# Row tiles of 128, column tiles, whole query loads, merged stores and a new tail in a cosformer and Hyena kernel

## The chip, the cores and the metric

The kernel runs on one core of a Trainium2 chip. The metric is the device time of one execution in microseconds. Runs that differ by over 1.5% from the fastest of the same kernel are called slow.

## The reference

Linear attention with a cosine weight, for 8 batches of 8 heads, 576 rows and 64 columns, and then a gate whose middle factor is a circular convolution along the rows:

```python
q_p, k_p = phi(q, cos_w, sin_w), phi(k, cos_w, sin_w)   # relu(x)*cos, relu(x)*sin side by side
kv  = einsum('bhsf,bhsd->bhfd', k_p, v);  z = k_p.sum(axis=2)
num = einsum('bhsf,bhfd->bhsd', q_p, kv)
den = einsum('bhsf,bhf->bhs', q_p, z)[..., None] + 1e-06
x   = (num / den) as (8, 576, 512)
x1, x2, x3 = split(x @ w_proj, 3)
x2_conv = irfft(rfft(x2, axis=1) * rfft(filter_fft, axis=0), axis=1)
out = (x1 * x2_conv * x3) @ w_out
```

## The kernel before

The batches are pipelined: while batch b goes through the gate, batch b + 1 gets its `num`, and batch b + 2 is loaded and prepared. Four rotating buffers serve the loads of q, k and v. From batch 2 on the prepared queries are transposed by DMA in four pieces, one for each pair of heads, so the `num` of a pair needs its own piece only. The x1/x3 input `xt` is a fifth transposing DMA. These and the stores of the output are issued from one engine, SyncE. (Cuts are marked with `# ...`.)

```python
def load_qk(b, nm, hs=slice(0, NH)):
    rw = work.tile([NP, NH, NJ * D], FP16, tag="raw", bufs=4, name=f"{nm}raw{b}")   # q, k and v
    # ... q from batch 2 on: three loads, the second half of each row with even and odd rows swapped

def emit_qt(b, hp):
    qp, qpt = qp_t[b], qpt_buf[0].rearrange("p (h n) -> p h n", h=NH)   # one qpt buffer
    hsl = slice(2 * hp, 2 * hp + 2)
    if b >= DMA_QT:
        nc.sync.dma_start_transpose(
            out=qpt[:, hsl].rearrange("p h (j n) -> p (h j) n", j=NJ),
            in_=qp[:, hsl].rearrange("p h j a b -> p (h j a b)"),
        )
        return
    # ... batches 0 and 1 on TensorE

def emit_x2(b, bls=range(3)):            # three blocks of 2 x 96 rows
    for bl in bls:
        u = unit(f"x2_{b}_{bl}")
        for comp in range(2):
            for c in range(NC):          # 8 matmuls of 96 rows x 512 columns
                nc.tensor.matmul(u[0:NP, comp], fx[:, c, ...], wp16[:, c, ds(DM, DM)], ...)
        # ... eviction on ScalarE

def emit_out(b, grps=OG):                # OT = [0, 128, 256, 384, 448]
    ov = out[b].rearrange("(k r) n -> r k n", r=12)
    # ... four matmuls for each 128 rows, eviction to os
            while pos < hi_:
                m = pos // 48
                e = min(hi_, (m + 1) * 48)       # a store has at most 48 rows of 2048 bytes
                k0, r = pos - m * 48, 6 * (m % 2) + m // 2
                q_ = nc.sync                     # ... some on other queues near the end
                q_.dma_start(out=ov[r, k0 : k0 + e - pos], in_=sv[pos - OT[t] : e - OT[t]])
                pos = e

for b in range(1, B + 1):                # n = b + 1
    # emit_x2(b, 0); num(n, 0), num(n, 1); emit_x2(b, 1); num(n, 2); dft; num(n, 3); emit_xt(n)
    # emit_x2(b, 2); dft; gates with folds of n; inverse transforms
    # loads of n + 1; phi of q (n + 1); the four emit_qt(n + 1); phi of k; copies of v
    # emit_out(b - 1); emit_kv(n + 1); emit_y(b)
```

## Time and profile before

| quantity | before |
|---|---|
| time, median of 3 runs | 254.21 us (251.4 to 259.21) |
| span of the profiled run, mean granted clock | 252.0 us, 0.970 |
| start (to the `kv` matmuls of batch 2) | 71.0 us |
| five batches, from one `kv` group to the next | 23.7, 25.0, 25.0, 25.0, 25.0 us |
| rest | 57.2 us |

The split into start, batches and rest is read from the timeline of TensorE: each batch begins its `kv` group once, and the distance of two groups (here called the pitch) is what a batch costs. The page's lines that show TensorE as the bound stand in the prediction.

First the DMA queue's own timeline for SyncE: start, time that the issue took, place, kind, transfer, count.

```profile
101.99 9.39 SPq L539 DMA_TRANSPOSE qpt<-qp  x3
111.47 4.82 SPq L617 DMA_TRANSPOSE xt<-att  x1
116.38 1.42 SPq L539 DMA_TRANSPOSE qpt<-qp  x1
```

Three of the four query pieces go ahead of `xt`, the last pair of heads behind it. The next batch's `num` begins at 122.98, and the `num` of that last pair only at 126.36, so the fourth piece has 10 us.

Second the transfers from 100 to 126 us, in 40 slices of 0.65 us: busy share of the 16 DMA engines in tenths, and GB/s.

```profile
DMA  7699999999669999999999199999999999999799
GB/s 145 39 153 221 185 143 135 235 315 214 52 133 285 238 167 89 92 187 200 236 133 68 13 215 285 291 290 224 194 189 186 184 247 32 335 413 271 44 120 162
```

Most slices are at 9: the engines are busy nearly all the time.

### The profile page before, as it was taken

Reading aid. Unit: us, or ns where it says so; the run is one execution under the profiler, and the core shown is the slowest. Engines: PE = TensorE matmul, PEld = TensorE weight load, DVE = VectorE, ACT = ScalarE, POOL = GpSimd, SP = SyncE. Lnnn points to the kernel's source line nnn. Section 1 sums busy time; section 2 is a strip of 40 time slices with the busy share of each in tenths; the row PEclk is TensorE's granted clock in tenths of the full one; section 3 lists DMA queues with packets and bytes.
Section 4 is the critical chain, followed back from the end, with each engine's and each line's share of the span. In section 5 each row is a group of like instructions: output and inputs, shape, how many; then the busy total and the mean of one; then the engine's idle time right before and its main releaser. Section 6 shows DMA issues by size and latency. Waiting matters only on the chain.

```text
span 252.0 us, 6140 instructions
## 1 busy us (share of the span) xinstructions
PE 226.1 (90%) x2313; PEld 159.9 (63%) x2313; DVE 210.4 (83%) x732; ACT 186.2 (74%) x281; POOL 38.1 (15%) x65
## 2 busy tenths in 40 slices
PE   0197897998988999999999999999999999999980
PEld 0067575655676867686768676867686778557730
DVE  7689899699779999999799979997998595828880
ACT  2244789799797876987698769876987488767720
POOL 8714211501501031103110311000000000000030
PEclk9997998899799999999999999999999999999996
DMA  5999999799999969999999999999982512153054
GB/s 68 167 205 205 207 200 153 101 166 196 173 121 157 169 56 202 174 176 194 200 225 143 141 217 199 137 183 156 161 197 53 153 41 58 44 146 83 3 153 140
DMA packets 74926, 37.30 MB, mean 148 GB/s; under 512 B 54288, under 2 KB 70160, under 8 KB 74896
## 3 DMA queue, kind: packets, MB, share of 16 engines
q0 software_dynamic: 26176, 17.21, 51.3%
q1 hardware_dynamic: 48320, 19.11, 40.6%
q10 hardware_dynamic: 400, 0.59, 0.7%
q8 instruction: 18, 0.29, 0.5%
q14 instruction: 12, 0.10, 0.2%
HBM read 33.69 MB, written 9.44 MB: 171 GB/s over the span
## 4 chain that ended last, share of the span: by engine, by line
PE 73%; DVE 13%; ACT 7%; DMA 3%; issue 1%; POOL 1%; POOLq 0%; DVEq 0%; ACTq 0%
PE x L674 21%; PE x L634 17%; PE out L752 12%; PE kv L527 5%; PE num L568 4%; PE fx L595 4%; PE dft L649 3%; DMA vraw<-in_v_dram 3%; PE inv L711 2%; PE inv L710 2%; DVE kp L104 2%; ACT va L142 1%; DVE eo L725 1%; DVE att L578 1%; PE qt L547 1%
## 5 line engine op out<-in xcount | busy, mean ns | idle before, releaser
L674 PE MATMUL x<-xt,wp 128*128 128x288 f16 x512 | 68.1, 286 | 0.0
L674 PEld LDWEIGHTS <-wp 128*128 128x128 f16 x512 | 48.9, 98 | 13.9 <-issue 0.9
L634 PE MATMUL x<-wp,fx 128*96 128x512 f16 x192 | 48.1, 395 | 1.6 <-DVE qpt L553 1.6
L752 PE MATMUL out<-wo,y 128*128 128x512 f16 x160 | 36.0, 379 | 0.1
L639 ACT ACTIVATE x2f<-x 96x1024 f16<-96x1024 f32 x24 | 24.5, 1020 | 14.2 <-PE x L634 13.9
L634 PEld LDWEIGHTS <-fx 128*96 128x96 f16 x192 | 23.0, 127 | 16.7 <-issue 3.7
L142 ACT COPY va<-vraw 96x768 f16<-96x768 f16 x32 | 25.2, 831 | 9.2 <-DMA vraw<-in_v_dram 9.2
L578 DVE TENSOR_TENSOR att<-num,rcp 96x768 f16<-96x768 f32 x32 | 30.3, 948 | 0.2
L752 PEld LDWEIGHTS <-y 128*128 128x128 f16 x160 | 15.3, 97 | 17.7 <-DVE y L730 0.6
L527 PE MATMUL kv<-va,kp 96*128 96x65 f16 x384 | 16.6, 199 | 10.2 <-ACT va L142 8.4
L684 ACT CAST x3s<-x 128x576 f16<-128x576 f32 x32 | 20.5, 641 | 5.9 <-PE x L674 5.9
L759 ACT ACTIVATE os<-out 128x1024 f32<-128x1024 f32 (+1 forms) x21 | 17.7, 880 | 9.0 <-PE out L752 8.7
L610 ACT CAST fx<-fx 128x576 f16<-128x576 f32 x32 | 20.6, 645 | 4.9 <-PE fx L595 4.9
L651 ACT CAST xf<-dft 96x1024 f16<-96x1024 f32 x24 | 24.2, 1008 | 0.0
L527 PEld LDWEIGHTS <-kp 96*128 96x128 f16 x384 | 15.1, 101 | 13.6 <-DVE kp L104 11.3
L699 DVE TENSOR_TENSOR g<-x3s,x1s 128x288 f16<-128x288 f16 x64 | 17.2, 299 | 6.8 <-ACT x3s L684 6.8
L681 ACT CAST x1s<-x 128x576 f16<-128x576 f32 x32 | 20.6, 645 | 1.8 <-PE x L674 0.8
L654 DVE TENSOR_TENSOR m<-xf,h 96x1024 f16<-96x1024 f16 x24 | 16.3, 681 | 6.1 <-ACT xf L651 5.1
L568 PEld LDWEIGHTS <-qpt 128*128 128x128 f16 (+1 forms) x384 | 16.2, 103 | 7.7 <-issue 3.9
L725 DVE TENSOR_TENSOR eo<-eq 128x288 f16<-128x288 f16 x64 | 17.5, 297 | 4.4 <-ACT eq L714 4.4
L595 PE MATMUL fx<-fm,att 96*128 96x96 f16 x240 | 17.0, 214 | 3.4 <-DVE att L578 1.7
L595 PEld LDWEIGHTS <-att 96*128 96x128 f16 x240 | 14.3, 101 | 7.6 <-DVE att L578 3.4
(192 smaller groups left out, 409.1 us busy)
## 6 DMA issues: line engine op xcount, KB each, us to landing
out_dram<-os SPq DMA_DIRECT2D x64, 96.0 KB, 2.2
kraw<-in_k_dram POOLq DMA_DIRECT2D x7, 576.0 KB, 8.6
vraw<-in_v_dram POOLq DMA_DIRECT2D x7, 576.0 KB, 8.9
qraw<-in_q_dram POOLq DMA_DIRECT2D x8, 288.0 KB, 6.0
qraw<-in_q_dram POOLq DMA_DIRECT2D x12, 144.0 KB, 5.9
wp<-in_moe_w_proj_dram POOLq DMA_DIRECT2D x3, 512.0 KB, 11.9
out_dram<-os SPq DMA_DIRECT2D x22, 64.0 KB, 2.2
out_dram<-os SPq DMA_DIRECT2D x23, 32.0 KB, 2.1
```

The lines of the kernel that those rows point to most:

```text
L142: nc.scalar.copy(out=va_buf[b % 2][:, hs, :, 0:D], in_=raw_t[(b, "v")][:, hs].rearrange("p h (j d) -> p h j d", j=NJ),)
L527: nc.tensor.matmul(u[:, h // 4, ds((h % 4) * 65, 65)], kp[:, j, h].rearrange("p a b -> p (a b)"), va[:, h, j, 0:65], start=(j == 0), stop= ...
L568: nc.tensor.matmul(u[0:m, hh, ds(t * 65, 65)], qpt[:, c0 : c0 + 2 * m - 1 : 2], kvs[:, h // 4, ds((h % 4) * 65, 65)], start=True, stop=True,)
L578: mark["att", b, hp] = nc.vector.tensor_tensor(out=att[:, :, ds(hp * 128, 128)].rearrange("p t (h d) -> p h t d", h=2), in0=nv[:, :, :, 0: ...
L595: nc.tensor.matmul(dst.rearrange("p (g e o) -> p g e o", e=2, o=8)[:, :, e], att[:, 2 * j + e, ds(c * 128, 128)], fm[0:NP, gs], start=True ...
L610: mark["fx", b] = nc.scalar.copy(out=dst[:, c].rearrange("p g (j o) -> p j g o", j=3), in_=uf[:, 0:768].rearrange("p (j g o) -> p j g o", ...
L634: nc.tensor.matmul(u[0:NP, comp], fx[:, c, ds(comp * 6 + 2 * bl, 2)].rearrange("p a b -> p (a b)"), wp16[:, c, ds(DM, DM)], start=(c == 0) ...
L639: mark["x2f", b, bl] = nc.scalar.mul(out=x2f[:, bl], in_=u[0:NP], mul=X2SC)
L651: mark["xf", b, bl] = nc.scalar.copy(out=xf, in_=u[0:NP])
L674: nc.tensor.matmul(u[:, hf, 0:HS], wp16[:, i, ds(w * DM + c * 128, 128)], xt[:, i, ds(6 * hf, 6)].rearrange("p a b -> p (a b)") if b < DMA ...
L681: mark["x1s", b, c] = nc.scalar.copy(out=x1s, in_=us[0][:, :, 0:HS])
L752: nc.tensor.matmul(u[:, x], y[:, c, ds(OT[t], 128)], wo16[:, c], start=(c == 0), stop=(c == NC - 1),)
```

## The change

The intent is to save TensorE time and to shorten the tail. x2 is computed in tiles of 128 rows, with the last 64 rows on two column halves of the array at once, and the DFT tables are padded to fit. The last 64 rows of the output are done on two column halves too. q is loaded whole into its own buffer with even and odd rows apart, and transposed in four 48-row pieces, each of which holds a part of every head. Half of the copies of v move to VectorE, and all of them later. The output's stores are merged to 96 rows where they can be, and the end of the last two batches is reordered.

```diff
+    q_buf = consts.tile([112, NH, NJ * D], FP16, tag="qraw", name="qraw")
-            rw = work.tile([NP, NH, NJ * D], FP16, tag="raw", bufs=4, name=f"{nm}raw{b}")
+            raw_t[(b, nm)] = q_buf if nm == "q" else work.tile(
+                [NP, NH, NJ * D], FP16, tag="raw", bufs=3, name=f"{nm}raw{b}"
+            )
... three loads of q become two, for even and odd rows
     def emit_qt(b, hp):
-        hsl = slice(2 * hp, 2 * hp + 2)
         if b >= DMA_QT:
+            e, half = hp % 2, hp // 2
             nc.sync.dma_start_transpose(
-                out=qpt[:, hsl].rearrange("p h (j n) -> p (h j) n", j=NJ),
-                in_=qp[:, hsl].rearrange("p h j a b -> p (h j a b)"),
+                out=qpt.rearrange("p h (j e m n) -> p (h j) e m n", j=3, e=2, m=2)[:, :, e, half],
+                in_=qp[ds(64 * ((e + half) % 2), 48), half].rearrange("p h j a b -> p (h j a b)"),
             )
... x2: two blocks of 8 matmuls with 128 rows, then
+                for c in range(2):
+                    for x in range(2):
+                        mm(u[ds(64 * x, 64), 0], 4, 64, c + 2 * x, range(2 * x, 2 * x + 2))
... DFT: nine matmuls on padded tables, not six; out: two column halves for the last 64 rows
-        ov = out[b].rearrange("(k r) n -> r k n", r=12)
+        ov = out[b].rearrange("(k x y) n -> x y k n", x=2, y=6)
-                    e = min(hi_, (m + 1) * 48)
+                    e = pos + 96 if pos % 96 == 0 and pos + 96 <= hi_ else min(hi_, (m + 1) * 48)
+                    if e - pos == 96:
+                        q_.dma_start(out=ov[:, m // 2], in_=sv[pos - OT[t] : e - OT[t]])
... order of the last batches
-            with behind("att", n, 1):
+            with behind(*("att", n, 3)):
                 emit_phi(n + 1, "k")
-                with behind(*(("x2f", b, x) if b > 1 else ("kvs", 2))):
-                    emit_va(n + 1, (2 * x, 2 * x + 1))
+                with behind("eo", b, 3):
+                    emit_va(n + 1, (0, 1))
+                with behind("g", b, 0):
+                    emit_va(n + 1, (2, 3), nc.vector.tensor_copy)
```

## The prediction

> **What bounds the kernel now.** I read the page's busy line and the chain that ended last, then the chain in order of time, which splits the run in three, then busy time by stage. Page first:
>
> ```profile
> PE 226.1 (90%) x2313; PEld 159.9 (63%) x2313; DVE 210.4 (83%) x732; ACT 186.2 (74%) x281; POOL 38.1 (15%) x65
> ...
> PE 73%; DVE 13%; ACT 7%; DMA 3%; issue 1%; POOL 1%; POOLq 0%; DVEq 0%; ACTq 0%
> ```
>
> TensorE holds 73% of the chain; the other engines' share lies at the two ends. The chain in order of time, one batch from the middle:
>
> ```profile
> 121.40 1.74 PE x L634 x8
> 123.14 0.79 PE num L568 x24
> 123.94 1.74 PE x L634 x8
> ...
> 126.92 1.75 PE x L634 x8
> ...
> 140.58 4.32 PE out L752 x20
> 144.90 1.53 PE kv L527 x48
> 146.42 1.74 PE x L634 x8
> ```
>
> A batch takes 146.42 - 121.40 = 25.02 us, every piece TensorE. A matmul of 512 columns costs 1.74/8 = 0.217 us. The work adds up: x2 24 x 0.217 = 5.2, DFT 6 x 0.216 = 1.3, gates 64 x 0.123 = 7.85 (16 in 1.96 in the chain), out 4.32, inverse 2.0, kv 1.53, num 1.58, folds 4 x 0.26 = 1.0, together 24.8. So TensorE has practically no bubble, and only fewer or shorter matmuls can help between 77 and 234 us. Busy time by stage, for two such batches, shows who is next:
>
> ```profile
> 121.40:146.42 25.02, 25.02 (x268) 18.00 (x266) 22.86 (x73) 20.84 (x30) 3.66 (x5) 1.00 1.24 178
> 146.42:171.44 25.02, 25.02 (x268) 17.99 (x266) 22.82 (x73) 20.79 (x30) 1.54 (x2) 1.00 1.21 176
> ```
>
> After the length come PE, weight loads, VectorE, ScalarE and GpSimd; then clock, DMA share, GB/s. VectorE is busy 22.8 of 25.0 us: a change can win about 2 us a batch before VectorE takes over. ScalarE has 4 us to spare. Before 77 us the chain mixes VectorE (30 to 42 us) and ScalarE (48 to 63 us); no PE saving counts there.
>
> At the end the timeline shows
>
> ```profile
> 240.67 0.46 DVE L730 TENSOR_TENSOR y<-y,g 128x576 f16<-128x576 f16 x1
> 241.18 3.35 PEld L752 LDWEIGHTS <-y 128*128 128x128 f16 x17 [0.59 <-DVE y L730]
> ...
> 245.06 0.69 DVE L102 TENSOR_SCALAR os<-out 128x512 f32<-128x512 f32 x1 [0.17 <-PE out L752]
> ```
>
> The last eviction ends at 245.75, yet the span is 252.0: 6.25 us of stores and ending. The stage table for 241 to 250 shows 111 to 271 GB/s, zero from 250 on. The transfers from 239 on are 1.84 MB, of which the last batch is 1.18: the rest are stores of the batch before, evicted as late as 239.6 to 241.1. The tail is limited by the stores' bytes, and about 2 us of ending follow.
>
> **What the Trainium skill says.** (1) "TensorE: Matmul & The Clock Gate", Back-to-back issue gap: N/2.4 + 2.5 ns when warm, 216 for 512 columns; the 0.217 agrees, and a matmul of 96 or 64 output rows costs as much as one of 128. That is what the 128-row tiles and column tiles use. (2) "TensorEngine Tiling (Array Packing)", Tiling Modes, Key Properties: tiles operate independently, but changing the tiling mode drains the engine. Before has a likely example of the drain, a weight of one column, here the weight-load timeline:
>
> ```profile
> 54.37 0.56 PEld L465 LDWEIGHTS <-hb 96*96 96x96 f16 x3
> 55.32 0.30 PEld L478 LDWEIGHTS <-alt 96*1 96x1 f16 x3 [0.40 <-issue]
> 56.06 0.12 PEld L649 LDWEIGHTS <-tre 96*96 96x96 f16 x1 [0.44 <-issue]
> ```
>
> Its load and the next one are not pulled ahead. Three matmuls from 54.58 should end issue at 55.23, h_nyq starts at 55.32; three more end at 55.97, DFT starts at 56.06. So I estimate 0.1 us a switch. That two 64-column tiles really overlap no record of before shows. (3) The clock-gate page, Part 3, "Measured speedup", gives 2.38x for three column tiles; I take nearly 2x for two. (4) "VectorE: DVE Perf Modes", perf-mode tier table: a 16-bit SBUF copy can run at 4x. The trace's like operation, the 96x768 maximum on q, takes 0.35 us.
>
> **The change part by part, per middle batch.**
>
> x2: three blocks of 8 matmuls become two of 8 and a 64-row rest in four matmuls, two on each half of the columns. The third block falls from 1.73 to 2 x 0.216 + 2 switches = 0.65, a gain of 1.08; without overlap it is 4 x 0.216 + 0.2 = 1.06, a gain of 0.67.
>
> DFT: six matmuls become nine (three outputs now cross two row tiles): a loss of 3 x 0.216 = 0.65.
>
> Out: the fifth tile's four matmuls of 512 (half their rows were repeats) become eight of 256 on two column halves. Overlapped 4 x 0.11 + 0.2 = 0.64 against 0.87, a gain of 0.2; otherwise 0.88 + 0.2, a loss of 0.2.
>
> Sum: 1.08 - 0.65 + 0.2 = 0.6 us a batch with overlap, 0.67 - 0.65 - 0.2 = -0.2 without. Batches 1 to 6 are in the TensorE stretch: **6 x 0.6 = 3.6 us**, or -1.1.
>
> Contiguous instead of strided query weights should give nothing: strided loads on qpt take 98 to 99 ns, contiguous ones on wp 98.
>
> ScalarE loses two v copies (2 x 0.83), 0.43 of x2 eviction and about 0.2 of out eviction, all off the path. VectorE gains the two copies, 0.7: 23.5 of 24.4, still not the bound, but with little room.
>
> Query: six loads' worth of 384-byte output runs become 768-byte, two issues instead of three; transposes stay four a batch, same bytes. Loads hide under 25 us of work today (the waits for DMA by VectorE or ScalarE are only the first v loads, 9.2 us), so zero. Each transpose now brings part of every head, so the first num matmul needs all four; but all four become ready together after the last num, so they should precede the x1/x3 transpose and arrive in time.
>
> Start: query 1 now shares query 0's only buffer, so its load is issued at about 24 us, when the second half of query 0 has been read (23.7), instead of 10.0. By then 4.5 MB have been issued and, at up to 205 GB/s, about 3.85 moved; a backlog of 0.67 plus its own 0.59 takes 6 us, so it lands at 30 to 31.5, and its first reader ran at 30.5. I charge 0.5 us. Seven memsets fit the 0.84 us that VectorE waits for the first iota; a few small operations add 0.3; ScalarE is 0.4 shorter. **Start: 0.4 us slower.**
>
> Tail: the previous batch's second store group moves ahead of the gates, inverse matmuls ahead of gate 2, and the last out tiles begin on three of four terms. Counting from the start of the last x2 (219.4), PE work to the end of the gates is 4.1 + 1.9 + 3.5 + 7.85 + 1.9 = 19.3, then eviction, two products: last y at about 21.5 against 21.7 now. After it, 14 matmuls (3.0 us), an eviction shared by two engines and merged stores whose queue now holds 1.3 MB and not 1.84. With about 230 GB/s that is 2.3 us less of stores at most; I expect 2.1. **Tail: 2.3 us.**
>
> Sum: 3.6 + 2.3 - 0.4 = 5.5; I add 1 us for what a tuned reordering gains that I can't see. 254.2 - 6.5 = **247.7 us**.
>
> **The rivals.** A: column tiles don't overlap, or each switch costs 0.25 us. Then the middle gives about nothing and only the tail is left: 252 us. For it: no overlap is in the trace. Against: the author pairs the tiles so that neighbours use different halves.
> B: VectorE becomes the bound. It has 23.5 us of work in 24.4; if copies behind the first gate delay the g products and the evictions behind them, half of the middle gain goes: 250 us. Its 1.39 us idle before num in each batch speaks against it.
> C: query 1 comes late and the whole VectorE chain from 30 us shifts by 2 to 3 us: 250 us. The DMA row is at 9 from the second slice, which speaks for it; the order of issue limits it.
> D: transposes late, num waits each batch by 1 us: 254 us. TensorE waits on no transpose now, but their landing takes 3.1 to 11.4 us.
> E: the start was also unlucky: three half-clock stretches of 3.4 us fell before 77 us, one on the first x2 (eight matmuls in 3.52 us). If they fall elsewhere it is worth 1 or 2 us either way.
>
> **Range and chances.** The three runs of before spread from 251.4 to 259.2, so the centre itself is loose by 2 us. Overlap with a good tail and a lucky start gives 243, A or D with a small tail gain 252. Faster by 2% means under 249.1: the centre is 1.4 us below it, chance 0.62. B, C and a weak tail fill the band to 2%, 0.35. Slower by 2% would need D and A together, 0.03.
>
> **What would show it.** The third x2 block in 0.6 to 0.7 us in the chain and not 1.7; out's last tile in 0.6; nine DFT matmuls; a batch of 24.4 us with the chain still TensorE; VectorE about 23.5 in it; the first use of query 1 with a wait under 1 us; after the last out eviction about 4 us of stores and ending, not 6.25. A batch of 25 us means A; waits of TensorE before num mean D; VectorE in the middle chain means B. The prediction is wrong if the tiles run one after another or if the start moves by over 2 us.

## The result

| | before | after |
|---|---|---|
| median (lowest to highest) | 253.63 us (251.4 to 259.21, 4 runs) | 297.13 us (293.9 to 302.89, 4 runs) |
| profiled run: span, mean clock | 252.0 us, 0.970 | 292.1 us, 0.922 |
| start | 71.0 us | 69.5 us |
| batches | 23.7, 25.0, 25.0, 25.0, 25.0 | 23.5, 24.1, 41.1, 31.0, 31.8 |
| rest | 57.2 us | 71.0 us |

The change is slower: ratio 1.1626, 95% interval 1.1472 to 1.178. A ratio here is the mean time of one kernel's fast runs over that of the other's of the same rounds, so it is not quite the ratio of the medians quoted, which are of all runs. The fast runs of the change took 293.9 and 294.12 us.

The 40 us between the two spans are 29 us in three of the five batches and 14 us in the rest, less 3 us won in the start and the first two batches. The busy line and the chain by engine of the page after:

```profile
PE 227.1 (78%) x2333; PEld 154.2 (53%) x2333; DVE 212.9 (73%) x751; ACT 178.4 (61%) x275; POOL 31.6 (11%) x55
...
DVE 32%; PE 23%; DMA 22%; ACT 11%; SPq 4%; issue 2%; ACTq 1%; POOL 0%; DVEq 0%; POOLq 0%
```

Hardly any engine has more work than before (TensorE 1.0 us, VectorE 2.5 us, the others less than before); TensorE fell from 73% of the chain to 23%, and transfers rose from 3% to 22%. What TensorE waits for shows its timeline at the start of the 41.1 us batch:

```profile
116.60 0.63 PE L813 MATMUL out<-wo,y 128*64 128x256 f16 x8
117.16 1.70 PE L550 MATMUL kv<-va,kp 96*128 96x65 f16 x48
118.69 1.89 PE L658 MATMUL x<-wp,fx 128*128 128x512 f16 x8
123.64 0.22 PE L594 MATMUL num<-kvs,qpt 128*128 128x65 f16 x1 [3.06 <-issue]
134.58 1.49 PE L594 MATMUL num<-kvs,qpt 128*128 128x65 f16 x23 [10.72 <-DMA qpt<-qp]
```

After one `num` matmul TensorE stands for 10.72 us, until a query transpose has landed. The list of waits gives the sum (us in total, times, longest), and SyncE's queue shows where that transpose stood:

```profile
PE num L594 <- DMA qpt<-qp: 21.6, 5, 10.7
```

```profile
108.45 8.15 SPq L564 DMA_TRANSPOSE qpt<-qp  x3
116.69 10.27 SPq L643 DMA_TRANSPOSE xt<-att  x1
127.01 4.69 SPq L564 DMA_TRANSPOSE qpt<-qp  x1
```

The order is that of before, three pieces, `xt`, one piece. But `xt` holds the queue for 10.27 us where it held it for 4.82, and the fourth piece, which now belongs to every head, is issued after the `num` that needs it. The same slices of DMA as before, 100 to 126 us, after:

```profile
DMA  9998111162112529991119999999999999999739
GB/s 226 218 219 143 42 35 41 35 152 52 39 43 82 155 70 152 123 53 50 49 44 215 245 281 70 126 167 180 154 197 175 241 154 86 112 189 169 21 58 196
```

This is the most telling view. While the merged stores are under way the digit is 1 and the rate 35 to 50 GB/s: work for one or two tenths of the engines, where before had nearly all at work. The Trainium skill, "DMA: Bandwidth & Descriptors", section "Why a DMA increments its semaphore by 16 and not by 1", says under "How many engines (k)" that a transfer is spread over the largest number up to 16 that divides the outermost dimension, leaving out those of size 1, of both sides. A merged store's destination is 2 x 48 rows of 512, so its outermost dimension is 2; a 48-row store's is 48. By that rule the merged store gets 2 engines and the other 16. The trace agrees: two engines of 16 are a share of 0.125. Counting the packets in the trace gives 84 ns (median) for one of 2048 bytes, hence 49 GB/s for two engines. The starts and durations of these packets say the same: exactly two of them were in flight for 64.5 us of the run after the change, and for 3.7 us before.

The tail's chain in order of time shows the same thing once more: ScalarE's output buffer is not free until stores of 7 and 8 us have landed.

```profile
245.19 7.12 DMA out_dram<-os
252.32 0.61 SPq L852
252.99 8.19 DMA out_dram<-os
```

### The profile page after: what moved, and what is told of

It reads as the page before. It is cut to its first block, busy times and chain, and to the rows that moved or that the text cites. A ratio compares the mean times of both kernels' runs of the same rounds, so it can differ in the third digit from the quotient of the medians.

```text
span 292.1 us, 6177 instructions
## 1 busy us (share of the span) xinstructions
PE 227.1 (78%) x2333; PEld 154.2 (53%) x2333; DVE 212.9 (73%) x751; ACT 178.4 (61%) x275; POOL 31.6 (11%) x55
## 3 DMA queue, kind: packets, MB, share of 16 engines
q0 software_dynamic: 21296, 16.85, 41.1%
## 4 chain that ended last, share of the span: by engine, by line
DVE 32%; PE 23%; DMA 22%; ACT 11%; SPq 4%; issue 2%; ACTq 1%; POOL 0%; DVEq 0%; POOLq 0%
DMA qpt<-qp 9%; PE x L723 7%; PE x L658 5%; DMA out_dram<-os 5%; DVE kp L107 5%; DVE att L604 4%; SPq L643 3%; DVE m L698 3%; DMA qraw<-in_q_dram 3%; PE num L594 3%; DVE m L699 3%; DMA xt<-att 3%; ACT va L144 2%; DVE eo L774 2%; DVE g L748 2%; DMA vraw<-in_v_dram 2%
## 5 line engine op out<-in xcount | busy, mean ns | idle before, releaser
L676 ACT ACTIVATE x2f<-x 128x1024 f16<-128x1024 f32 (+1 forms) x24 | 21.2, 884 | 48.7 <-PE x L658 48.7
L658 PE MATMUL x<-wp,fx 128*128 128x512 f16 (+1 forms) x160 | 39.8, 413 | 1.7 <-DVE qpt L580 1.0
L594 PE MATMUL num<-kvs,qpt 128*128 128x65 f16 (+1 forms) x384 | 19.6, 208 | 26.9 <-DMA qpt<-qp 21.6
L594 PEld LDWEIGHTS <-qpt 128*128 128x128 f16 (+1 forms) x384 | 17.9, 109 | 34.5 <-DMA qpt<-qp 20.9
L600 DVE TENSOR_TENSOR rcp<-num,epsc 96x12 f32<-96x12 f32 x32 | 5.1, 161 | 36.3 <-PE num L594 36.3
L795 PE MATMUL out<-wo,y 128*128 128x512 f16 (+1 forms) x132 | 30.3, 379 | 0.0
L695 ACT CAST xf<-dft 96x1024 f16<-96x1024 f32 x24 | 24.1, 1004 | 2.1 <-PE dft L690 2.0
L144 ACT COPY va<-vraw 96x768 f16<-96x768 f16 x24 | 18.7, 845 | 8.8 <-DMA vraw<-in_v_dram 8.8
L636 ACT CAST fx<-fx 128x576 f16<-128x576 f32 x32 | 20.5, 641 | 4.6 <-PE fx L621 4.6
L658 PEld LDWEIGHTS <-fx 128*128 128x128 f16 (+1 forms) x160 | 13.7, 106 | 17.0 <-issue 6.6
L730 ACT CAST x1s<-x 128x576 f16<-128x576 f32 x32 | 20.5, 640 | 1.7 <-PE x L723 0.7
L795 PEld LDWEIGHTS <-y 128*128 128x128 f16 (+1 forms) x132 | 12.4, 98 | 14.6 <-issue 1.0
L839 ACT ACTIVATE os<-out 128x1024 f32<-128x1024 f32 x14 | 14.3, 1032 | 8.6 <-DMA out_dram<-os 5.6
```

The source lines that it names most:

```text
L144: copy(out=va_buf[b % 2][:, hs, :, 0:D], in_=raw_t[(b, "v")][0:NP, hs].rearrange("p h (j d) -> p h j d", j=NJ),)
L594: nc.tensor.matmul(u[0:m, hh, ds(t * 65, 65)], qpt[:, ds(h * S + t * NP, m)], kvs[:, h // 4, ds((h % 4) * 65, 65)], start=True, stop=True,)
L658: nc.tensor.matmul(dst, fx[:, c].rearrange("p g o -> p (g o)")[:, ds(128 * ch, n)], wp16[:, c, ds(DM, DM)], start=(c == cs[0]), stop=(c == ...
L676: mark["x2f", b, bl] = nc.scalar.mul(out=x2f[:, 2 * bl : 2 * bl + n], in_=u[:, 0:n], mul=X2SC)
L695: mark["xf", b, bl] = nc.scalar.copy(out=xf, in_=u[0:NP])
L795: nc.tensor.matmul(us[t], y[:, c, ds(OT[t], nr)], wo16[:, c], start=(c == 0), stop=(c == NC - 1),)
```

## The experiments

In the expectations, S is the theory that the merged stores cost, T that it costs to need all four query pieces before `num`, and L that loads get bunched. All kernels gave the right result. "Before" in the table is the median of the kernel before on the same chip in the same rounds. The medians are of all runs, slow ones too; the comparisons below use the fast runs and the ratios. Where the last column is empty, a kernel had one fast run only. e17 has one too, its profiled run; its ratio leaves that run out and is of the three others, which count as slow beside it.

| run | this, us | its fast runs, us | before, us | ratio (95% interval) |
|---|---|---|---|---|
| e4_merge_only | 297.18 | 295.94 to 297.91 (4) | 252.4 | 1.176 (1.1642 to 1.1878) |
| e12_merge_on_act | 301.92 | 295.69 | 253.08 | |
| e1_store48 | 267.06 | 264.62, 265.47 | 252.4 | 1.0491 (1.036 to 1.0622) |
| e2_order | 290.22 | 289.31 to 291.87 (4) | 252.4 | 1.1495 (1.1395 to 1.1594) |
| e3_both | 268.44 | 266.98 to 268.97 (3) | 252.4 | 1.0606 (1.0499 to 1.0713) |
| e5_va_act | 257.19 | 255.55 to 257.93 (4) | 251.87 | 1.0159 (1.0024 to 1.0295) |
| e7_no_query | 245.1 | 244.2 to 246.65 (4) | 251.87 | 0.97 (0.9589 to 0.9811) |
| e8_query_only | 263.28 | 259.87, 262.3 | 251.87 | 1.0326 (1.0124 to 1.0529) |
| e9_no_q_no_va | 250.38 | 249.88 to 250.43 (3) | 251.87 | 0.9892 (0.973 to 1.0054) |
| e10_all_heads | 257.34 | 244.65 | 253.08 | |
| e11_query_4bufs | 266.02 | 257.97 | 253.08 | |
| e13_query_by_heads | 263.17 | 261.15 to 264.72 (4) | 252.68 | 1.0438 (1.0344 to 1.0533) |
| e14_query_order | 259.05 | 255.05, 258.27 | 252.68 | 1.0185 (1.0068 to 1.0302) |
| e15_48_by_heads | 265.55 | 262.64 to 266.52 (3) | 252.68 | 1.0499 (1.0361 to 1.0637) |
| e16_query_heads_order | 253.93 | 253.05 to 256.45 (4) | 253.68 | 1.0073 (0.9995 to 1.0151) |
| e17_all_mended | 257.87 | 253.52 | 253.68 | 1.0243 (1.0159 to 1.0326) |
| e18_again | 245.99 | 243.93 to 246.76 (4) | 253.68 | 0.9714 (0.9645 to 0.9783) |
| e19_heads_late | 266.57 | 263.05, 265.48 | 253.42 | 1.0574 (1.048 to 1.0668) |

### The stores

**e4_merge_only**: the kernel before with nothing but the merged stores.

```diff
-        ov = out[b].rearrange("(k r) n -> r k n", r=12)
+        ov = out[b].rearrange("(k x y) n -> x y k n", x=2, y=6)
-                    e = min(hi_, (m + 1) * 48)
+                    e = pos + 96 if pos % 96 == 0 and pos + 96 <= hi_ else min(hi_, (m + 1) * 48)
```

> The kernel before with one edit: its 48-row stores are merged into 96-row stores where the changed kernel does so (three per batch), nothing else. Theory S: clearly slower, 270 to 290 us, with waits for transposes on TensorE. Theory T: within 2% of the kernel before, 254 us.

It took 297.18 us, as much as the whole change. Median landing of a query transpose rose from 7.1 to 13.3 us, and `num` waited 18.9 us in all for them. The merged stores alone are enough for the whole loss.

**e12_merge_on_act**: e4, with the merged stores issued from ScalarE's queue, so that the transposes no longer stand behind them.

```diff
-                        q_.dma_start(out=ov[:, m // 2], in_=sv[pos - OT[t] : e - OT[t]])
+                        nc.scalar.dma_start(out=ov[:, m // 2], in_=sv[pos - OT[t] : e - OT[t]])
```

> The kernel before with the merged 96-row stores, as in the run that had this alone (297 us), but with these stores issued from ScalarE's queue in place of SyncE's. If the stores cost because they stand ahead of the transposes in one queue, 253 to 258 us. If they cost because a merged store is spread over too few DMA engines (about 33 us of work on two engines for a loaded batch by estimate), moving the queue doesn't help: 275 us or more, with transposes landing late still.

(The estimate of 33 us is a count of packets: 288 packets of merged stores a batch, at 84 ns on two engines, are 12.1 us; these engines' share of transposes, loads and other stores comes to 7.8, 11.4 and 1.5 us.) It took 295.69 us in its one fast run, as much as e4. From 100 to 126 us only two slices fall to digit 1, but the rate is low again, 35 to 65 GB/s in nine slices:

```profile
DMA  9995468999984931179999999999999999999999
GB/s 224 214 268 165 89 61 89 156 200 215 214 152 110 150 37 39 35 46 56 65 55 51 63 143 240 239 83 83 174 180 190 164 83 242 151 91 89 88 89 54
```

The transposes are still slow, with no merged store in their queue: from 107 us on four query pieces held SyncE for 17.28 us and `xt` for 13.87 (before: 10.81 and 4.82), and in a later batch of 34.0 us the chain waits 16.77 us for `xt` to land. So a place behind the merged stores is not needed to delay them. But the longest stall of e12, in a batch of 45.1 us, goes another way:

```profile
121.48 17.01 ACTq L772 DMA_DIRECT2D out_dram<-os  x2
138.53 0.59 ACT L533 CAST kvs<-kv 128x520 f16<-128x520 f32 x1 [20.06 <-DMA qpt<-qp]
139.17 1.58 PE L568 MATMUL num<-kvs,qpt 128*128 128x65 f16 x24 [18.24 <-ACT kvs L533]
```

ScalarE stood for 17.01 us at the issue of two merged stores, so its copy of `kvs` came late, and `num` waited 18.24 us for that copy. The issue ended as SyncE's `xt` issue did (138.23); why it took so long is not shown. The total time of e12 therefore does not settle how much of e4's loss is the place in the queue. What fits all of this is that two engines have to do a batch's merged stores, and every transpose or load that uses all engines is done only when these two are. The last clause is an inference from the landing times.

**e1_store48**: the changed kernel with stores of 48 rows again; the order of SyncE's transposes is pinned to what the change has.

```diff
-                    e = pos + 96 if pos % 96 == 0 and pos + 96 <= hi_ else min(hi_, (m + 1) * 48)
+                    e = min(hi_, (m + 1) * 48)
```

> The changed kernel with one edit: its 96-row output stores (three per batch, destination of two interleaved groups of 48 rows) are issued as pairs of 48-row stores; the order of the transposes on the SyncE queue is pinned to that of the changed kernel (three query pieces, the x1/x3 transpose, fourth query piece). Theory S (the 96-row stores move on few DMA engines, drip out over some 15 us and hold back the transposes behind them): about 250 us, no wait of TensorE before num over 1 us, 2048-byte packets gone within 6 us of their issue. Theory T (the fourth query piece is queued behind the x1/x3 transpose, and num now needs all four): stays above 280 us.

265 us in the fast runs: 29 of the 41 us come back, less than theory S expected. But TensorE still waits 20.5 us for query transposes, in two stalls. (This profile is of a slow run, 271.7 us; a fast run of e15, below, which also has 48-row stores, shows 14.4 us of such waits.) A second cause lies beneath the first.

### The order in the queue

**e2_order** (merged stores kept) and **e3_both** (48 rows) put all four query pieces ahead of `xt` (the edit is shown against e1, whose order is pinned):

```diff
-                if b > 1 and x == 2:
+                if b > 1 and x == 3:
                     with behind("sp"):
                         emit_xt(n)
```

> The changed kernel with its 96-row stores, but the fourth query transpose is issued before the x1/x3 transpose in every batch. Theory T: the waits of TensorE on the query transpose vanish, about 250 us. Theory S: still over 280 us, because the query pieces themselves wait behind the stores.

> Both edits. Both theories together: about 247.7 us, the prediction's own sum (a batch of 24.4 us, tail 2 us shorter). If it stays over 255 us a third cause is at work.

e2 took 290.4 us and e3 268.0 (means of the fast runs): the order alone wins about 4 us with merged stores (294.0 without it) and nothing with stores of 48 rows (265.0 without it). In e3 `xt` took the place of the query pieces: it landed 18.8 us after its issue, and `num` still waited 13.9 us.

**e5_va_act** is e3 with the copies of v on ScalarE and the k part as early as before:

```diff
-            with behind(*("att", n, 3)):
+            with behind(*("att", n, 1)):
                 emit_phi(n + 1, "k")
-                with behind("eo", b, 3):
-                    emit_va(n + 1, (0, 1))
-                with behind("g", b, 0):
-                    emit_va(n + 1, (2, 3), nc.vector.tensor_copy)
+                with behind(*(("x2f", b, x) if b > 1 else ("kvs", 2))):
+                    emit_va(n + 1, (2 * x, 2 * x + 1))
```

> As the run with both edits (48-row stores, fourth query transpose ahead of the x1/x3 transpose), and the v copies and the k products go back to where the kernel before has them (all four copies on ScalarE behind the x2 evictions, k behind the second att). Theory L (half of the v copies now sit on VectorE at the end of the gates, hold the v buffer until there, and so bunch the v, k and q loads of the next batch right on top of the transposes): 248 to 253 us, x1/x3 transposes landing in under 11 us and no longer 18. Theory Q (transposes of 48 rows are slow in themselves): unchanged, 265 to 268.

257.19 us, with one batch of 30.6 us left. With the query part in place, the late copies and the late k part together cost 11 us.

### The query part

**e7_no_query** is the changed kernel with 48-row stores and before's query part (loads, four shared buffers, pieces by heads); all else, late copies too, is as changed. **e9_no_q_no_va** takes the late copies back as well. **e8_query_only** is the kernel before with the query part alone.

```diff
-            e, half = hp % 2, hp // 2
+        hsl = slice(2 * hp, 2 * hp + 2)
... and the loads, phi of q and the query weights of num, each as in the kernel before
```

> The changed kernel with 48-row stores and with the query part taken back (loading in three pieces, four shared raw buffers, transposes by heads of 96 rows), the late v copies kept. Theory Q: 247 to 250 us. Theory L: still over 258, since the late v copies stay; less if the fourth shared buffer spreads the loads.

> The changed kernel with 48-row stores, without the query part and without the late v copies: what remains is x2 in 128-row tiles, column tiles and the new tail. By the prediction's sum for these parts 254 - 3.6 - 2.3 = 248 us, with a batch of 24.4 us. Both theories agree here; over 255 means a third cause.

> The kernel before with the query part alone (whole load, own buffer, 3 shared buffers for k and v, 48-row transposes). Theory Q: 262 us or more. Theory L: within 2% of the kernel before.

e7 took 245.1 us, faster than both kernels. Its chain in order of time, one batch:

```profile
116.83 1.73 PE x L647 x8
118.56 0.80 PE num L583 x24
119.36 1.73 PE x L647 x8
...
121.48 0.67 PE dft L679 x3
122.15 0.40 PE num L583 x12
122.55 0.55 PE x L647 x4
123.10 0.78 PE dft L679 x3
```

The third x2 block takes 0.55 us for four matmuls on two column halves, where four in a row would be 4 x 0.217 = 0.87: the tiles overlap. Busy time of two batches (length, PE, weight loads, VectorE, ScalarE, GpSimd, clock, DMA share, GB/s):

```profile
91.10:115.30 24.20, 24.20 (x274) 17.08 (x271) 24.03 (x76) 19.15 (x29) 2.74 (x4) 1.00 1.06 178
115.30:139.50 24.20, 24.20 (x274) 17.08 (x272) 23.55 (x76) 19.15 (x29) 3.54 (x6) 1.00 1.07 178
```

TensorE has no gap again, in a batch of 24.2 us; VectorE is close behind. In e9 one batch took 29.3 us, with waits for query transposes, in a run with a span of 248.7 us. The ratios are 0.9892 for e9 and 0.97 for e7: here the late copies of v help, which they did not in e5's pair.

e8's fast runs took 259.87 and 262.3 us, about 8 us over before. Its 48-row transposes are not slow in themselves: they land in 7.7 us at the median, before's in 7.1. The stall of its 30.8 us batch, in the timelines of TensorE and SyncE's queue:

```profile
121.93 0.19 PE L579 MATMUL num<-kvs,qpt 128*128 128x65 f16 x1
126.04 0.91 PE L579 MATMUL num<-kvs,qpt 128*128 128x65 f16 x23 [3.92 <-DMA qpt<-qp]
```

```profile
113.72 6.92 SPq L628 DMA_TRANSPOSE xt<-att  x1
120.70 1.35 SPq L549 DMA_TRANSPOSE qpt<-qp  x1
```

The fourth piece is issued at 120.70 and lands after 5.3 us; `num` would have had its turn at 121.9. Before, such a piece was needed at 31.6 us of a batch (126.36 - 94.7) and issued at 21.7; here it is needed at 28.3 (121.93 - 93.7) and issued at 27.0. The first difference is the need for all heads. The second is the queue, where three pieces and `xt` took 17.9 us against 14.2, and began 1.7 us later.

**e10_all_heads** turns this round: e7 with pieces of 96 rows that each hold all heads.

> The kernel without the query part, in which the four query transposes of a batch are cut another way: two 96-row pieces that each cover all heads, in place of four that each cover two heads. Loads, number of bytes and the rest stay as they were. Theory T (the first num matmul of a batch must now wait for the last piece, where before it waited only for its own heads) expects stalls on DMA qpt<-qp before num and a median of 250 us or more. The rival, that the query part costs through its loads and shared buffers alone, expects 244 to 247 us and no such stalls.

Three runs of 256 to 259 us stand against one of 244.65, and by the rule the three count as slow. The profiled one of them has a wait of 9.4 us for a query transpose, but a difference that only slow runs show proves nothing. Inconclusive.

**e11_query_4bufs** is e8 with four shared buffers for k and v in place of three (memory for it came from the last outputs' buffers).

```diff
-                [NP, NH, NJ * D], FP16, tag="raw", bufs=3, name=f"{nm}raw{b}"
+                [NP, NH, NJ * D], FP16, tag="raw", bufs=4, name=f"{nm}raw{b}"
```

> The kernel before with the query part alone, but with four shared buffers for the loads of k, v and q in place of three (the room comes from the last batch's output buffers, two in place of five, which can lengthen the tail; so the pitch of the middle batches is read). Theory L (the loads run into one another for want of a free buffer) expects middle batches of 25 us again, no stalls of num on the query transposes, and 252 to 256 us. Theory T expects the pitch to stay uneven (one or two batches of 27 to 31 us) and 258 us or more.

Its one fast run took 257.97 us, e8's fast runs 259.87 and 262.3; the tail had fewer buffers too. No sign that a fourth buffer cures it, but one run is no proof. (The same idea for the whole changed kernel was not run.)

**e13_query_by_heads** cuts e8's pieces in two by heads; **e14_query_order** puts e8's four pieces ahead of `xt`; **e16_query_heads_order** does both.

```diff
-            e, half = hp % 2, hp // 2
-            nc.sync.dma_start_transpose(
-                out=qpt.rearrange("p h (j e m n) -> p (h j) e m n", j=3, e=2, m=2)[:, :, e, half],
-                in_=qp[ds(64 * ((e + half) % 2), 48), half].rearrange("p h j a b -> p (h j a b)"),
-            )
+            e, hsl = hp % 2, slice(4 * (hp // 2), 4 * (hp // 2) + 4)
+            for half in range(2):
+                nc.sync.dma_start_transpose(
+                    out=qpt[:, hsl].rearrange("p h (j e m n) -> p (h j) e m n", j=3, e=2, m=2)[:, :, e, half],
+                    in_=qp[ds(64 * ((e + half) % 2), 48), half, hsl].rearrange("p h j a b -> p (h j a b)"),
+                )
```

> The kernel before with the query part alone, but each 48-row transpose cut in two by heads, so that the first four of eight pieces hold all of heads 0 to 3 and num can begin on these; bytes, loads, order of the queue and the whole load of q stay. Theory T (all heads wait for the last piece) expects an even pitch near 25 us, little or no wait of num on the query transposes, and 251 to 255 us, against 263 with the query part as it was. The rival (whole load of q, or 48-row pieces slow in themselves) expects 258 us or more.

> The kernel before with the query part alone, with all four query transposes ahead of the x1/x3 transpose of the batch in SyncE's queue, and nothing else changed. If only the place of the fourth piece behind the x1/x3 transpose costs, 252 to 256 us. If the stall comes with any need for all four pieces, because they follow each other closely and land late when a load shares the engines, 257 to 262 us with one or two stalls left, or new stalls of x1/x3 on its transpose.

> The kernel before with the query part alone, the 48-row transposes cut by heads and all of them ahead of the x1/x3 transpose. If the cost of the query part is only the lost slack before num (which pieces it needs, and where the last of them stands), the pitch is even near 25 us, num waits under 2 us in all for the query transposes, and 251 to 255 us. If a stall of 4 us or more stays, something else delays the pieces (the loads that share the engines), and it stays at 257 us or more.

e13 missed its expectation: 263.17 us, ratio 1.0438 against e8's 1.0326, so no better than e8. TensorE's timeline shows why:

```profile
150.44 0.93 PE L580 MATMUL num<-kvs,qpt 128*128 128x65 f16 x24
151.21 1.91 PE L646 MATMUL x<-wp,fx 128*96 128x512 f16 x8
158.65 1.13 PE L580 MATMUL num<-kvs,qpt 128*128 128x65 f16 x12 [5.54 <-DMA qpt<-qp]
```

Heads 0 to 3 ran at once at 150.44, but the third pair of heads waited: three of the eight pieces still stood behind `xt`, issued at 149.65. The stall had only moved. e14's fast runs took 255.05 and 258.27 us: a little under half of e8's cost is back (ratio 1.0185 against 1.0326, with intervals that overlap). e16, both together, took 253.93 us against 253.68 (ratio 1.0073, at most 1.0151), with a pitch of 23.7, 25.0, 25.0, 26.4 and 25.0 us and no wait of `num` for a transpose in its profile. So on the kernel before, the query part's cost is the lost slack of the pieces: which heads they hold, and where the last of them stands.

### Both mends in the changed kernel

**e15_48_by_heads** is e1 with e13's cut; **e17_all_mended** is e5 with it; **e19_heads_late** is e3 with it. **e18_again** times e7 once more.

> The changed kernel with 48-row stores and with the 48-row query transposes cut in two by heads (both causes mended, all else as in the change). If the two causes are all of the loss, 244 to 250 us; with the late copies of v bunching the loads as a third cause, 252 to 262 us with uneven pitch; 265 us or more would mean that cutting by heads does nothing here (267 with 48-row stores alone).

> The changed kernel with 48-row stores, v copies and k phi as before, all query transposes ahead of the x1/x3 transpose (257 us so far), and now these cut by heads too. If nothing else is wrong with the change, 246 to 251 us and an even pitch near 24.5 us; if loads on the same engines still make pieces late, 254 us or more with one batch of 28 to 31 us.

> The changed kernel with 48-row stores and query transposes cut by heads and ahead of the x1/x3 transpose; v copies and k phi late, as the change has them. If the late copies are good whatever the query part does, 245 to 250 us, and no stall over 2 us. If late copies, three shared buffers for k and v and a single one for q bunch the loads (as in the run with both mends and late copies, 268 us), stalls of 4 us or more stay and it is 256 us or more.

> The same kernel as the one without the query part and with 48-row stores (245.1 us), timed again in five rounds, as the best version: 244 to 247 us, 2.5 to 3.5% under the kernel before, in every run.

None comes near e7. In their fast runs e15 took 262.64 to 266.52 us and e19 263.05 and 265.48. e17 has one fast run, 253.52 us, level with before; its three others took 257.58 to 260.11. The profile of that fast run still has one batch of 30.8 us, in which `num` waits 4.3 us for a query transpose. In the changed kernel the two mends are not enough. In e19 it is now the last in the queue, `xt`, that comes late, in the chain of waits, while GpSimd issues three loads of 576 KB within 9 us:

```profile
146.36 17.56 DMA xt<-att
```

```profile
141.28 1.98 POOL L139 DMA_DIRECT2D vraw<-in_v_dram  x1 [19.28 <-DVE va L144]
145.35 0.77 POOL L139 DMA_DIRECT2D kraw<-in_k_dram  x1 [2.09 <-ACT va L144]
149.73 1.24 POOL L137 DMA_DIRECT2D qraw<-in_q_dram  x2 [3.61 <-DVE qp L107]
```

The load of v waits for the late copies to free its buffer. e7 has the same bunch (v at 134.56, q at 138.31, k at 143.02) and no stall; there `xt` goes first (127.56), and the pieces by pairs of heads follow it. Why the same loads hurt in one and not in the other is not settled: `xt` first with pieces by heads in the changed kernel was not tried. So what the query part does in the changed kernel is shown only as a whole, by taking it back (e7). The safe version is e7: in e18, five rounds more, 245.99 us, ratio 0.9714.

## Why the prediction was wrong

It said 247.7 us, faster at 0.62, and gave slower 0.03. It came out at 297.

- **The step that failed first: the stores.** The prediction priced "merged stores" by their bytes, with "about 230 GB/s", and only in the tail, where it expected 2.3 us of gain from all of the tail's changes. It never asked over how many engines a store of this form is spread. Two engines do it at 35 to 50 GB/s. This term, put at a gain, costs 45 us alone (e4), both in the batches and in the tail, which grew by 14 us. The section that says so is not among the four places that the prediction cites.
- **The second: the query part.** "So zero" and "they should precede the x1/x3 transpose and arrive in time" were both wrong: the fourth piece stands behind it, as the fourth did in the trace of before. It costs about 8 us alone (e8), and on the kernel before e16 shows that it is this slack.
- **Rival D had the mechanism and not the size.** It named waits before `num` and put them at 1 us a batch, 254 us in all. The trace shows 21.6 us in five waits. That it went with "D and A together" for slower left out that waits for transfers can grow without A.
- **Costs do not add.** In fast runs: merged stores alone +44, query part alone +8, the whole change +41, although its remainder is worth -7 (e7). That both causes delay the same transposes, and TensorE waits once, would explain it; no run tests it.
- **What was right: the middle.** x2's third block took 0.55 us (predicted 0.65), out's last tile 0.56 (0.64), so rival A is out. DFT's nine matmuls took 0.67 + 0.78 + 0.65 = 2.10 us, 0.8 above before's 1.3 (predicted 0.65 above). A quiet batch takes 24.2 us, predicted 24.4. VectorE has 23.6 to 24.0 us in it, predicted 23.5; its copies of v took 0.35 us each, as predicted. Rival B did not come, but it is the next bound.
- **The tail, with 48-row stores.** In e7 the part after the last pitch fell from 57.2 to 54.3 us, in e18 to 54.5: 2.7 to 2.9, predicted 2.3. The last eviction ends at 238.57 of 242.5, so about 4 us follow, as predicted.
- **The start.** 69.5 us against 71.0. One wait of VectorE of 3.0 us for the load of q is there, where "under 1 us" was expected; the start did not grow by it. Rival C did not come.

## What to carry to other kernels

Before two stores are merged into one, look at the outermost dimension of both sides: a small number there can leave the transfer to that many engines, and other transfers of the core can then run late behind it. Moving the issue to an engine that computes can stop that engine's work at the issue (17.01 us in e12). When pieces of a transfer are cut another way, ask for each consumer which piece it needs last and what stands ahead of that piece in its queue. A pipelined kernel with no gap on its bound engine hides how little slack its transfers have; read it from the timeline before counting a transfer as hidden.

## What the Trainium skill lacked or had wrong

- "DMA: Bandwidth & Descriptors", "Why a DMA increments its semaphore by 16 and not by 1": its rule for the number of engines agrees with the trace. It lacks what follows for other transfers: with three stores of 192 KB a batch on two engines the median landing of the transposes rose from 7.1 to 13.3 us (e4).
- "TensorE: Matmul & The Clock Gate", Part 3, "Measured speedup": the table has no pair of tiles of 64 columns. Here four such matmuls took 0.55 us and not 0.87 (4 x 0.217), a speedup of 1.6 with whatever the switches of mode cost (the prediction's "nearly 2x" with two switches of 0.1 us gave 0.65 us, 1.3).
- No page was found to say how long the issue of a DMA holds its engine while other transfers run. Here one `xt` held SyncE for 4.82 us before and 10.27 us after, one 48-row query piece for 1.35 us (e8) to 4.69 us (after), and two merged stores held ScalarE for 17.01 us (e12).
